# Expert rows gathered in four pieces and turned on VectorE, in a fused attention and mixture-of-experts kernel

## The chip, the cores and the metric

The kernel runs on one core of a Trainium2 chip. The metric is the device time of one execution in microseconds (us). Five engines work beside each other and meet through semaphores: TensorE (PE; its weight loads are listed as PEld), VectorE (DVE), ScalarE (ACT), GpSimd (POOL) and SyncE (SP, which only issues transfers). Each engine runs its own instructions strictly in the order written. Transfers issued by SP, ACT and POOL share 16 DMA engines.

## The reference

```python
# q, k, v, f_logit: (4, 8, 768, 48); w_gate: (384, 8); w1: (8, 384, 1024); w2: (8, 1024, 384)
f = 1 / (1 + exp(-f_logit))
for t in range(S):                     # per batch and head
    state = f[t][:, None] * state + outer(k[t], v[t])
    y[t] = q[t] @ state
x = y.transpose(0, 2, 1, 3).reshape(3072, 384)

logits = x @ w_gate
# all (token, expert) pairs by falling logit: a token goes to the expert if it has
# none yet and the expert has fewer than 384 tokens
for e in range(8):
    out[assigned == e] = relu(x[assigned == e] @ w1[e]) @ w2[e]
```

All inputs and outputs are fp32. Each of the eight experts ends with exactly 384 tokens, that is three tiles of 128 rows.

## The kernel before

**Attention.** 24 chunks of 128 tokens go through a software pipeline whose order is written out by hand (`stages`, `drain`, `finale`). For each chunk the result `x` (128 tokens by 384 features) is written with its eight logits to a table `xd` in DRAM: one row per token, `DX` = 392 columns. POOL copies the logits into the row (`with_logits`, L369), and a store follows (`store`, L374), on SP's queue for 21 chunks and on ACT's for the last three. The steps called through `later(step, ...)` set constants up beside the pipeline.

**The first assignment.** `search` finds, digit by digit, the logit above which each expert takes its first choices. Before it starts, the weights of experts 0 and 1 are asked for (`load_weights`, L576); the small copy before each load ("behind") keeps the load from starting early.

**Lists.** `positions`, `numbers` and `sort` turn the choices into lists of token numbers: a sort is 24 matmuls against one-hot tiles. The list of expert 0's first two tiles is made alone (`tok0`, L895); two indirect DMAs on POOL's queue gather those rows (`fetch`, L769). Then POOL copies `blk` (L900), and VectorE and TensorE make all other lists (`found`, `tok`, L902 to L904). POOL gathers the logits of the tokens left over (`lg`, L914, six transfers) and then the first two tiles of experts 1 to 4 (L920). `idle_turns` are matmuls on constants whose result nobody reads.

**Experts and search, interleaved.** `ffn(e, first_block, n)` gives a list of TensorE pieces: `turn` transposes a row tile by three matmuls into PSUM (L704) and copies it to `xT` (L708, ScalarE except for one tile); `up` makes H = w1 x and its Relu (L716, L720); `down` makes O from `hT` and w2 (L730), copies it (L735) and scatters it to the output with an indirect DMA (L736). At the Relu of `ft` 1 and 6, `up` also asks for the weights of the expert after next. `add` puts the transposes of the next expert among the last down pieces of the one before, `AHEAD_OF` from the end. The pieces stand in a queue `pe_work`. The assignment of the tokens left over (six rounds of `search_rest`, four digits each, with a count on TensorE at L805 and short VectorE operations) is written down beside it: `V` adds a planned duration to VectorE's clock, and `PE` pops pieces until TensorE's planned clock has passed VectorE's, and only then writes the count. So the interleaving is fixed when the program is built, by planned durations. First come two tiles each of experts 0 to 4, under the search; then the third tile of each; then experts 5 to 7 with three tiles each.

Of the kernel before, what the change touches and what calls it, by code (L numbers as in the profile page):

```python
# [25 lines left out]
def kernel(  # L26
# [11 lines left out]
    nc = tc.nc  # L38
# [36 lines left out]
    DX = D + E  # L75
# [292 lines left out]
    def with_logits(G):  # L368
        nc.gpsimd.tensor_copy(out=G["x"][:, D:DX], in_=logits[:, G["b"] * NCH + G["c"]])  # L369

# [85 lines left out]
    later(3, lambda: make_upper_triangular(nc, upper[:], val=1.0, diag=False))  # L456
    later(4, lambda: nc.vector.tensor_copy(out=linef[:], in_=line_i[:]))
# [111 lines left out]
    def load_weights(e, pool, slot, parts=(0, 1), behind=None):  # L569
        for part in parts:  # L570
            shape, src = (([128, DC, F], moe_w1), ([128, FC, D], moe_w2))[part]
            w = pool.tile(shape, FP32, name=f"w{part + 1}", tag=f"w{part + 1}_{slot}", bufs=1)
            if behind is not None:
                (nc.gpsimd.tensor_copy if e < 2 else nc.scalar.copy)(
                    out=w[0:1, 0, 0:1], in_=behind)
            nc.sync.dma_start(out=w[:], in_=src[e].rearrange("(c p) f -> p c f", p=128))  # L576
            slots.setdefault(e, [None, None])[part] = w
# [72 lines left out]
    with tc.manual_schedule(engines=FIXED):  # L650
        for load, n in ((load_f, 0), (load_k, 0), (load_q, 0), (load_f, 1), (load_v, 0), (load_k, 1),
                        (load_q, 1), (load_f, 2), (load_v, 1)):
            load(chunks[n])
        load_gate()
        for z in range(2):
            nc.sync.dma_start(out=mask[HC * z:HC * z + HC, 1], in_=mask[HC - HC * z:C - HC * z, 0])
        attention(-1, ALL)
        for e in range(2):
            load_weights(e, early, e, behind=chunks[-1]["y0"][0:1, 0, 0:1])
        base = search(over0[:], choice0, NT)  # L660
# [4 lines left out]
    def fast():  # L665
# [28 lines left out]
        def ffn(e, first_block, n, ahead=None):  # L694
# [5 lines left out]
            def turn(i):  # L700
                def go():
                    X = bank("Xe", "H")
                    for d in range(DC):
                        nc.tensor.transpose(out=X[:, 128 * d:128 * d + 128],  # L704
                                            in_=rows[e, first_block + i][:, 128 * d:128 * d + 128],
                                            identity=ident[:])
                    copy = nc.vector.tensor_copy if first_block + i == 1 and e == 0 else nc.scalar.copy
                    copy(out=xT[:, :, 128 * i:128 * i + 128],  # L708
                                   in_=X[:, 0:D].rearrange("p (c t) -> p c t", t=128))
                return 0.65, go  # L710

            def up(ft, d):
                def go():
# [5 lines left out]
                    if d == DC - 1:  # L719
                        nc.scalar.activation(out=hT[:, ft, 0:w], in_=L["H"][:, 0:w], func=AF.Relu)  # L720
                        if ahead is not None and ft in (1, 6):
                            load_weights(ahead, pools[ahead], ahead, (ft // 6,),
                                         hT[0:1, ft, 0:1])
# [23 lines left out]
        AHEAD_OF = 3  # L747
# [18 lines left out]

        def fetch(e, i):
            t = work.tile([128, DX], FP32, name="xe", tag="xe", bufs=10)
            nc.gpsimd.indirect_dma_start(  # L769
                out=t[:], out_offset=None, in_=xd[:, :],  # L770
                in_offset=bass.IndirectOffsetOnAxis(ap=token(e, i), axis=0))
            rows[e, i] = t
# [108 lines left out]
        with tc.manual_schedule(engines=engines):  # L881
# [6 lines left out]
            idle_turns(12, "A")  # L888
            p0 = place_of(0, 0)
            r, in_line = sort(line, numbers(blk, value[:], blocks[:, p0:p0 + 2], NT, 2), NT, 2, 4)  # L890
            idle_turns(20, "A")
# [4 lines left out]
            for i in range(2):  # L896
                lists[0, i] = tok0[:, i:i + 1]
                fetch(0, i)
            blk_all = rt([NT], "blk_all", FP16, 1)
            nc.gpsimd.tensor_copy(out=blk_all[:], in_=blk[:])  # L900
            r, _ = sort(line, numbers(blk_all, value[:], blocks[:], NT, NQ), NT, NQ, 12, in_line)
# [5 lines left out]
               float(1024 * (DX // E) + D // E), ALU.add)  # L907
            for e in range(1, NA):
                for i in range(2):
                    p = place_of(e, i)  # L910
                    lists[e, i] = tok[:, p:p + 1]
# [9 lines left out]
            idle_turns(3, "A")  # L921

            clock.update(pe=4.0, dve=0.0)
            for e in range(NA):
                add(ffn(e, 0, 2, e + 2 if e + 2 < NA else None))
                if e == 0:
                    for _ in range(8):
                        piece()

            val_l = rt([NL], "val_l", FP16, 1)  # L930
            nc.vector.tensor_copy(out=val_l[:], in_=found[:, 0:NL])
# [17 lines left out]
            clock["dve"] = 16.8  # L949
# [46 lines left out]
            numb2 = numbers(blk2, val_l[:], blocks[:, NL:NQ, 0:NL], NL, NQ - NL)  # L996
# [5 lines left out]
            ts(tok2[:], sum2[:], 1024.0, ALU.add)  # L1002
            for e in range(E):
                for i in range(2 if e < NA else 0, TE):
                    p = place_of(e, i) - NL
                    lists[e, i] = tok2[:, p:p + 1]
# [30 lines left out]
            for e in range(NA, E):  # L1037
                at = max(0, len(pe_work) - 28)
                pe_work.insert(at, (0.0, lambda e=e: [fetch(e, i) for i in range(TE)]))
# [427 lines left out]
```

## Time and profile before

| What | Value |
|---|---|
| Time, median of 3 runs | 438.8 us (438.66 to 438.98) |
| The profiled execution | 441.33 us, span 439.5 us |
| Mean granted TensorE clock | 0.971 |
| PE busy | 419.9 us, 4576 instructions |
| DVE busy | 184.1 us, 621 instructions |
| POOL busy | 109.7 us, 235 instructions |
| Indirect DMA to gather row tiles (L769) | 24, 966 ns each on POOL |
| Transposes of row tiles on PE (L704) | 72 |
| Attention | to about 139 us |
| First expert matmul (L716) | 164.55 us |

The span runs from the first to the last instruction of the profiled execution. A line in a group names source line, engine, operation, output and input; behind it stand the count, the busy time and the mean duration, and then what the engine waited for before it. The chain of waits is followed back from the last instruction: each step names what released it. The granted clock is the share of full speed that TensorE was given. Busy time on PE is no measure of the work in it, because matmuls overlap: a duration in the chain counts, one in a group is longer.

### The profile page before, as it was taken

What the parts mean: (1) busy time and instruction counts of PE and PEld (TensorE: products, weight loads), DVE (VectorE), ACT (ScalarE), POOL (GpSimd) and SP (SyncE); (2) the same over time, 40 slices, a digit from 0 to 9 for tenths busy, and PEclk for the clock granted to TensorE, in tenths of its full rate; (3) what the DMA queues carried; (4) which work ended last, traced back from release to release, by engine and by line L of the source; (5) the groups of instructions that cost most, each with busy time, mean ns of one, the idle gap of its engine ahead of it and who ended that gap; (6) DMA issues with size and microseconds to landing.
All of it is one profiled execution on the core that took longest, in us unless ns stands there. A gap on an engine that the chain in (4) does not pass through costs nothing.

```text
span 439.5 us, 11007 instructions
## 1 busy us (share of the span) xinstructions
PE 419.9 (96%) x4576; PEld 305.1 (69%) x4576; DVE 184.1 (42%) x621; ACT 157.5 (36%) x370; POOL 109.7 (25%) x235
## 2 busy tenths in 40 slices
PE   7899999999999879999999999999999999999991
PEld 3678888788787558686767777788886556556550
DVE  5598888888898822366666640000000000000000
ACT  3677777677763102121312122232222212203200
POOL 4344444444432037300001032100033014010010
PEclk9999999999999588999999999999999999999997
DMA  9899998798893954845260013079932102000010
GB/s 156 141 175 178 187 190 181 167 185 182 175 195 104 398 206 146 307 148 171 91 221 36 1 42 89 36 244 294 318 104 67 38 18 70 22 18 36 1 37 22
DMA packets 119147, 59.31 MB, mean 135 GB/s; under 512 B 102320, under 2 KB 113712, under 8 KB 119088
## 3 DMA queue, kind: packets, MB, share of 16 engines
q1 hardware_dynamic: 115392, 48.35, 44.0%
q0 software_dynamic: 3264, 9.56, 6.8%
q8 instruction: 38, 0.62, 0.6%
q10 hardware_dynamic: 432, 0.60, 0.4%
q14 instruction: 21, 0.17, 0.2%
HBM read 48.91 MB, written 9.54 MB: 133 GB/s over the span
## 4 chain that ended last, share of the span: by engine, by line
PE 69%; issue 15%; DMA 6%; DVE 3%; POOL 3%; ACT 2%; SPq 0%; POOLq 0%; DVEq 0%
PE H L716 23%; PE O L730 21%; PE T L234 4%; DMA w<-in_moe_w_dram 4%; PE A L276 3%; PE L L171 3%; PE Y L306 3%; PE L L361 2%; PE T L344 2%; PE small L255 2%; PE Xe L704 2%; PE Y L317 1%; POOL out_dram L736 1%; DMA q<-in_q_dram 1%; PE small L199 1%
## 5 line engine op out<-in xcount | busy, mean ns | idle before, releaser
L716 PE MATMUL H<-xeT,w 128*128 128x256 f32 (+2 forms) x624 | 132.7, 370 | 0.8 <-issue 0.8
L730 PE MATMUL O<-w,hT 128*128 128x384 f32 x384 | 132.6, 490 | 0.0
L716 PEld LDWEIGHTS H<-xeT,w 128*128 128x128 f32 x624 | 100.4, 193 | 27.7 <-ACT xeT L708 1.1
L730 PEld LDWEIGHTS O<-w,hT 128*128 128x128 f32 x384 | 69.7, 190 | 39.2 <-issue 0.2
L736 POOL DMA_INDIRECT out_dram<-o,tok x24 | 23.3, 970 | 211.5 <-ACT o L735 206.1
L720 ACT ACTIVATE hT<-H 128x256 f32<-128x256 f32 (+2 forms) x104 | 38.2, 367 | 91.3 <-PE H L716 87.9
L735 ACT COPY o<-O 128x384 f32<-128x384 f32 x24 | 11.5, 478 | 74.5 <-PE O L730 73.0
L284 DVE COPY_PREDICATED am<-mask,A 128x512 f32<-128x512 int32 x48 | 34.6, 724 | 0.2 <-PE A L276 0.2
L708 ACT COPY xeT<-Xe 128x384 f32<-128x384 f32 x23 | 11.0, 478 | 55.5 <-PE Xe L704 55.5
L769 POOL DMA_INDIRECT xe<-xd,tok x24 | 23.2, 966 | 19.7 <-DMA w<-in_moe_w_dram 12.7
L276 PE MATMUL A<-qT,kT 48*64 48x128 f32 (+1 forms) x768 | 22.3, 251 | 0.4 <-ACT kT L242 0.3
L171 PE MATMUL L<-g,wcum 128*128 128x384 f32 x48 | 19.7, 491 | 1.0 <-ACT g L167 1.0
L306 PE MATMUL Y<-am,v 64*64 64x64 f32 (+1 forms) x368 | 19.8, 243 | 0.0
L276 PEld LDWEIGHTS A<-qT,kT 48*64 48x64 f32 x768 | 18.7, 133 | 1.4 <-ACT kT L242 0.5
L157 POOL COPY w<-v 64x256 f32<-64x256 f32 x48 | 18.9, 394 | 2.5
L306 PE MATMUL Y<-am,w 64*64 64x128 f32 (+1 forms) x368 | 19.2, 243 | 0.0
L306 PEld LDWEIGHTS Y<-am,v 64*64 64x64 f32 x368 | 17.9, 134 | 0.0
L234 PE MATMUL T<-ident,qg 128*128 128x128 f32 x96 | 15.8, 285 | 2.2 <-DVE qg L187 2.0
L344 PEld LDWEIGHTS T<-ident,yT 128*128 128x128 f32 x92 | 11.6, 150 | 8.8 <-ACT qT L242 5.6
L209 POOL TENSOR_TENSOR gl<-span,spans 128x4 f32<-128x4 f32 x20 | 3.9, 196 | 54.2 <-DVE span L206 33.2
L306 PEld LDWEIGHTS Y<-am,w 64*64 64x64 f32 x368 | 17.3, 134 | 0.0
L176 DVE TENSOR_SCALAR dl<-L 128x384 f32<-128x384 f32 x24 | 13.3, 554 | 8.8 <-PE L L171 8.4
(238 smaller groups left out, 543.4 us busy)
## 6 DMA issues: line engine op xcount, KB each, us to landing
w<-in_moe_w_dram SPq DMA_DIRECT2D x16, 1536.0 KB, 7.8
f<-in_f_logit_dram SPq DMA_DIRECT2D x24, 192.0 KB, 4.2
k<-in_k_dram SPq DMA_DIRECT2D x24, 192.0 KB, 5.1
q<-in_q_dram SPq DMA_DIRECT2D x24, 192.0 KB, 4.9
v<-in_v_dram SPq DMA_DIRECT2D x24, 192.0 KB, 4.8
xd<-x SPq DMA_DIRECT2D x21, 196.0 KB, 4.5
xd<-x ACTq DMA_DIRECT2D x3, 196.0 KB, 6.4
xe<-xd,tok POOLq DMA_INDIRECT x24, 3.5
```

What stands on the lines that cost most here:

```text
L157: nc.gpsimd.tensor_copy(out=w[HC * z:HC * z + HC], in_=G["v"][HC - HC * z:C - HC * z, H // 2:H])
L171: nc.tensor.matmul(out=G["Lv"], lhsT=wcum[:], rhs=g_bufs[G["i"] % NB][:, :, 0:DH], start=True, stop=True)
L234: nc.tensor.transpose(out=t[:, 128 * hp:128 * hp + 128], in_=G[src][:, 2 * hp:2 * hp + 2, :].rearrange("t h d -> t (h d)"), identity=ident[:])
L276: nc.tensor.matmul(out=A[par][to, 128 * hp + first * j:128 * hp + 128], lhsT=G["kT"][rows, hp, HC * j:HC * j + HC], rhs=G["qT"][rows, hp, ...
L284: nc.vector.copy_predicated(am[:, par].rearrange("s (a b) t -> s a b t", b=2), mask[:].unsqueeze(2).to_broadcast((128, 2, 2, 128)), A[par] ...
L306: nc.tensor.matmul(out=G["Y"][r0][DP * r:DP * r + DP, 128 * blk + first:128 * blk + 128], lhsT=v, rhs=G["am"][rows, h % 2, h // 2, first:128],
L344: nc.tensor.transpose(out=X[:, 128 * hp:128 * hp + 128], in_=G["yT"][:, hp, :], identity=ident[:])
L716: nc.tensor.matmul(out=L["H"][:, 0:w], lhsT=slots[e][0][:, d, 128 * ft:128 * ft + 128], rhs=xT[:, d, 0:w], start=(d == 0), stop=(d == DC - 1))
L720: nc.scalar.activation(out=hT[:, ft, 0:w], in_=L["H"][:, 0:w], func=AF.Relu)
L730: nc.tensor.matmul(out=L["O"][:, 0:D], lhsT=hT[:, ft, 128 * i:128 * i + 128], rhs=slots[e][1][:, ft, :], start=(ft == 0), stop=(ft == FC - 1))
L736: nc.gpsimd.indirect_dma_start(out=outs[next(tiles)][:, :], out_offset=bass.IndirectOffsetOnAxis(ap=token(e, first_block + i), axis=0), in ...
L769: nc.gpsimd.indirect_dma_start(out=t[:], out_offset=None, in_=xd[:, :], in_offset=bass.IndirectOffsetOnAxis(ap=token(e, i), axis=0))
```

## The change

A row tile is no longer gathered as 128 whole rows. The table's rows become 480 columns wide, five pieces of 96: four pieces of features and one of logits, the eight logits repeated twelve times, so that a row can be addressed in pieces. For a tile, four indirect DMAs fetch 128 pieces each. A new list (`quadrants`: four short matmuls with `perm` and one VectorE operation) names for each partition the token and the piece: in gather g, partition 32a + r gets piece a of token 32g + r. Then VectorE's transpose, which works within blocks of 32 by 32, gives the full transpose of the tile in four instructions (`by_blocks`). The features land in the order 3p + d, so the first weights are loaded with three neighbouring rows on a partition ("(p c) f"). Expert 0's first two tiles are still gathered whole and transposed by matmul (`by_matmul`), in the same order of features, and are worked on one after the other instead of together. The lists of all others are made from `blk` directly, without POOL's copy, before expert 0's transposes. The numbers of idle turns, `AHEAD_OF`, the planned start of the search (16.8 to 14.0) and the places of the later fetches change with it, and the copies before weight loads touch all 128 partitions.

```diff
-    DX = D + E
+    PW = D // 4
+    DX = 5 * PW
...
-        nc.gpsimd.tensor_copy(out=G["x"][:, D:DX], in_=logits[:, G["b"] * NCH + G["c"]])
+        nc.gpsimd.tensor_copy(
+            out=G["x"][:, D:DX].rearrange("t (n e) -> t n e", e=E),
+            in_=logits[:, G["b"] * NCH + G["c"]].unsqueeze(1).to_broadcast((128, PW // E, E)))
...
+    perm = const([128, 4, 128], FP16, "perm")
+    first_piece = const([128, 1], FP32, "first_piece")
+    for a in range(4):
+        later(8 + a, lambda a=a: nc.gpsimd.memset(first_piece[32 * a:32 * a + 32], 5120.0 + a))
+        later(9 + a, lambda a=a: nc.gpsimd.tensor_copy(
+            out=perm[:, a].rearrange("p (b r) -> p b r", r=32),
+            in_=ident[:, 32 * a:32 * a + 32].unsqueeze(1).to_broadcast((128, 4, 32))))
...
-                    out=w[0:1, 0, 0:1], in_=behind)
-            nc.sync.dma_start(out=w[:], in_=src[e].rearrange("(c p) f -> p c f", p=128))
+                    out=w[:, 0, 0:1], in_=behind)
+            nc.sync.dma_start(out=w[:], in_=src[e].rearrange(
+                "(p c) f -> p c f" if part == 0 else "(c p) f -> p c f", p=128))
...
             def turn(i):
-                def go():
-                    X = bank("Xe", "H")
+                def by_matmul():
+                    X = [bank("Xe", "H"), bank("Xe2", "O")]
+                    x = rows[e, first_block + i][:, 0:D].rearrange("t (p d) -> t d p", d=DC)
                     for d in range(DC):
-                        nc.tensor.transpose(out=X[:, 128 * d:128 * d + 128],
-                                            in_=rows[e, first_block + i][:, 128 * d:128 * d + 128],
-                                            identity=ident[:])
-                    copy = nc.vector.tensor_copy if first_block + i == 1 and e == 0 else nc.scalar.copy
-                    copy(out=xT[:, :, 128 * i:128 * i + 128],
-                                   in_=X[:, 0:D].rearrange("p (c t) -> p c t", t=128))
-                return 0.65, go
+                        nc.tensor.transpose(
+                            out=X[d > 0][:, 128 * d:128 * d + 128], in_=x[:, d],
+                            identity=ident[:])
+                    nc.vector.tensor_copy(out=xT[:, 0, 0:128], in_=X[0][:, 0:128])
+                    nc.scalar.copy(out=xT[:, 1:DC, 0:128],
+                                   in_=X[1][:, 128:D].rearrange("p (c t) -> p c t", t=128))
+
+                def by_blocks():
+                    x = rows[e, first_block + i][:, 0:D].rearrange(
+                        "t (g c d) -> t g d c", g=4, d=DC)
+                    for g in range(4):
+                        nc.vector.transpose(
+                            out=xT[:, :, 128 * i + 32 * g:128 * i + 32 * g + 32], in_=x[:, g])
+                    V(4, 0.25)
+
+                return (0.65, by_matmul) if e == 0 and first_block < 2 else (0.0, by_blocks)
...
-        AHEAD_OF = 3
+        AHEAD_OF = 8
...
         def fetch(e, i):
-            t = work.tile([128, DX], FP32, name="xe", tag="xe", bufs=10)
-            nc.gpsimd.indirect_dma_start(
-                out=t[:], out_offset=None, in_=xd[:, :],
-                in_offset=bass.IndirectOffsetOnAxis(ap=token(e, i), axis=0))
-            rows[e, i] = t
+            if e == 0 and i < 2:
+                t = rows[e, i] = work.tile([128, DX], FP32, name="x0", tag="x0", bufs=2)
+                nc.gpsimd.indirect_dma_start(
+                    out=t[:], out_offset=None, in_=xd[:, :],
+                    in_offset=bass.IndirectOffsetOnAxis(ap=token(e, i), axis=0))
+                return
+            t = rows[e, i] = work.tile([128, D], FP32, name="xe", tag="xe", bufs=7)
+            for g in range(4):
+                nc.gpsimd.indirect_dma_start(
+                    out=t[:, PW * g:PW * g + PW], out_offset=None,
+                    in_=xd[:, :].rearrange("n (a x) -> (n a) x", x=PW),
+                    in_offset=bass.IndirectOffsetOnAxis(ap=quads[e, i][g], axis=0))
+
+        def quadrants(found16, n, name):
+            PE(0.1)
+            r = bank("quad", "r")
+            for g in range(4):
+                nc.tensor.matmul(out=r[:, g * n:g * n + n], lhsT=perm[:, g], rhs=found16,
+                                 start=True, stop=True)
+            q = rt([4, n], name, I32, 1)
+            ts(q[:].rearrange("p g n -> p (g n)"), r[:, 0:4 * n], 5.0, ALU.mult,
+               first_piece[:, 0:1], ALU.add)
+            return q
...
-            idle_turns(12, "A")
+            idle_turns(11, "A")
...
-            idle_turns(20, "A")
+            idle_turns(6, "A")
...
-            blk_all = rt([NT], "blk_all", FP16, 1)
-            nc.gpsimd.tensor_copy(out=blk_all[:], in_=blk[:])
-            r, _ = sort(line, numbers(blk_all, value[:], blocks[:], NT, NQ), NT, NQ, 12, in_line)
+            r, _ = sort(line, numbers(blk, value[:], blocks[:], NT, NQ), NT, NQ, 12, in_line)
...
+            found16 = rt([NQ], "found16", FP16, 1)
+            nc.vector.tensor_copy(out=found16[:], in_=found[:])
+            idle_turns(6, "A")
+            quad = quadrants(found16[:], NQ, "quad")
+            idle_turns(6, "A")
...
-            idle_turns(3, "A")
-
             clock.update(pe=4.0, dve=0.0)
             for e in range(NA):
-                add(ffn(e, 0, 2, e + 2 if e + 2 < NA else None))
-                if e == 0:
-                    for _ in range(8):
+                ahead = e + 2 if e + 2 < NA else None
+                if e:
+                    add(ffn(e, 0, 2, ahead))
+                else:
+                    add(ffn(e, 0, 1, ahead))
+                    add(ffn(e, 1, 1))
+                    for _ in range(16):
                         piece()
...
-            clock["dve"] = 16.8
+            clock["dve"] = 14.0
...
+            sum16 = rt([NQ - NL], "sum16", FP16, 1)
+            nc.vector.tensor_copy(out=sum16[:], in_=sum2[:])
+            V(4)
+            quad2 = quadrants(sum16[:], NQ - NL, "quad2")
...
             for e in range(NA, E):
-                at = max(0, len(pe_work) - 28)
-                pe_work.insert(at, (0.0, lambda e=e: [fetch(e, i) for i in range(TE)]))
+                for i in range(TE):
+                    at = max(0, len(pe_work) - 64 + 12 * i)
+                    pe_work.insert(at, (0.0, lambda e=e, i=i: fetch(e, i)))
                 add(ffn(e, 0, TE))
```

## The prediction

> **What bounds the kernel now.** I read the page's busy times first, then the chain of work that ended last, then the granted clock microsecond by microsecond where the chain leaves TensorE, then VectorE's groups.
>
> The busy times of the span of 439.5 us:
>
> ```profile
> PE 419.9 (96%) x4576; PEld 305.1 (69%) x4576; DVE 184.1 (42%) x621; ACT 157.5 (36%) x370; POOL 109.7 (25%) x235
> ```
>
> The chain, in order of time (start, length, what):
>
> ```profile
> 140.23 15.94 DMA w<-in_moe_w_dram
> 156.32 1.18 POOL xe L769
> 157.81 0.95 POOL xe L769
> ...
> 160.16 1.51 PE tokens L874 x24
> 161.68 0.84 PE nothing L106 x3
> 162.52 1.28 PE Xe L704 x6
> 163.80 0.75 issue
> 164.55 4.78 PE H L716 x12
> ...
> 291.78 5.36 PE H L716 x48
> 297.13 3.87 PE O L730 x12
> 301.33 1.29 PE O L730 x4
> 302.63 5.36 PE H L716 x48
> ```
>
> From 164.55 us on, the chain is TensorE alone: every TensorE piece taken out shortens the kernel by its length, if nothing else becomes late. Between 140 and 164.55 us it is a hand-over: weight loads and the last stores of rows, the first gather, the sort that gives all other lists, then the six transposes. An fp32 matmul stands as two records, a transpose as one. The expert from 291.78 to 302.63 takes 10.85 us: 5.35 us for 24 up matmuls (223 ns each), 16 down records at 3.87/12 = 0.3225 us, that is 5.16 us, and a rest of 0.33 us: the three transposes of the next tile, put among the down matmuls.
>
> TensorE by microsecond (busy and count, granted clock, DMA share, GB/s):
>
> ```profile
> 158.00:159.00 1.00, 0.20 (x2) 1.00 1.09 356
> ...
> 161.00:162.00 1.00, 1.00 (x16) 0.83 0.01 3
> ...
> 168.00:169.00 1.00, 1.00 (x5) 0.75 0.07 2
> ```
>
> TensorE has nothing from 158.2 to 160.16; the clock falls to half in 161 and is full again only in 168. The first 12 up records therefore take 398 ns each, later ones of this width 227 (8 in 1.82 us): 2.05 us lost.
>
> VectorE's groups by form (count | busy, mean ns | idle before):
>
> ```profile
> L206 DVE STREAM_TRANSPOSE span<-small 128x128 f32<-128x128 f32 x24 | 7.4, 308 | 0.0
> L426 DVE TENSOR_SCALAR full_r<-cnt,there 128x32 f32<-128x32 f32 x24 | 6.0, 251 | 23.8 <-PE cnt L805 23.8
> ...
> L816 DVE STREAM_TRANSPOSE turned<-most_r 128x32 f32<-128x32 f32 x24 | 5.1, 211 | 0.8
> ```
>
> In the search (180 to 258 us) VectorE waits for TensorE, 23.8 us over 24 digits, mostly 0.43 us each: that is the room for more VectorE work.
>
> **The change part by part.** The sum is made against the span of 439.5 us; the profiled execution itself took 441.33 us, the median of the runs shown is 438.8, so I take the difference from 438.8.
>
> *Transposes off TensorE.* Of 24 row tiles, two (expert 0's first two) are still transposed by matmul. 22 x 0.33 us = 7.3 us leave the chain: eight tiles of experts 1 to 4, five third tiles, nine of experts 5 to 7. Their ScalarE copies go too (478 ns each, off the chain). **-7.3.**
>
> *VectorE's side.* Four transposes of 128x96 a tile. Between the two rows (211 ns for 32 columns, 308 for 128) one is about 275 ns; independent instructions start closer than their length (0.12 us apart at 200.10 and 200.22, of 0.21 us), so a tile takes 0.85 to 1.1 us; the planner counts 1.0. Eight tiles fall into the search, in four pairs, and the planner puts more TensorE pieces before each next count. Cost 0; without that room the bound is 8 x 0.1 = 0.8, and if the reads with a step of three elements cost double, 32 x 0.25 = 8 less 4 x 4 x 0.43 = 7 of room around the pairs, so about 1. After 260 us VectorE is idle.
>
> *Four gathers a tile.* An indirect DMA holds POOL 0.95 us, the next starts 0.3 later, whatever the row size: 1.25 us. Rows are gathered by POOL in the order lg, experts 1 to 4, and only then the scatters. With lg from about 159.4 us (below), six lg end at 166.9, eight pieces for expert 1 start until 175.6, and land 2.6 later in quiet (lg: 2.2 to 3.3), 7.3 at most beside a weight load (the slowest xe): 178 to 183. Who waits: VectorE's transposes of expert 1 stand behind round 1's sums, and behind them stand the next round's operations, its count on TensorE, and expert 1's matmuls. By TensorE's order the round's fourth count comes at 179.5 us (162.5, 24 ups 5.36, transposes 0.33, 8 downs 5.16, 2 + 21 ups 5.1, four counts 0.6, the rest waits), the sums 2.5 later at 182, expert 1's first matmul at 185. So the gathers are there or about 1 late, with 1 us of room: I take +0.3, between 0 and +1.5. Experts 2, 3, 4 have their pieces by 189, 199, 209 us and start at about 208, 230, 252. The scatters of expert 0 wait until POOL is through, 207 us: then three o buffers are held, and the fourth ScalarE copy (208 us) waits some 1.5 us, behind it the Relu of expert 2; three banks of H cover 2 us: 0. Of the later lists, expert 0's third tile is nearest: from the second quadrant product 0.5 us to the list, 3.75 to the fourth issue, 2.9 to land and turn, 7.5 in all, against 16 downs = 10.3 us: 0, with 3 us left.
>
> [...] The row first: lg's 32-byte rows land in 2.2 to 3.3 us, xe's 1568-byte rows in 3.0 at best, so small pieces are not slower here. [...] I take 0.
>
> *A full list beside the first gathers.* Before, the all-lists product waits for POOL's small copy behind both gathers (158.76), and expert 0's transposes stand behind it on TensorE. After, VectorE forms it from 155.33 to 156.5, the sort is through at 158.0, the lists at 158.9, the quadrant product, and TensorE is free at about 160.5 after 12 idle turns. The end is then the first gather: it lands 4.9 us after its issue at 156.32. That issue waited for the last row store (token list ready at 155.3, so 0.7 us is the store's); a store is 480 columns instead of 392, 22% more: its 6.6 us to landing grow by 0 to 1.45, I take 0.4, since the weights queued with it set most. Landing 161.6; one transpose, the small VectorE copy (about 0.3) and hand-overs make the first up matmul 162.5 instead of 164.55: 2.05 us, less 0.33 for the second tile's transposes now inside. **-1.7** (0 to -3).
>
> *The clock.* By the rows above, 2 us without a matmul and then 1.5 us of narrow ones sufficed for half clock. After, the longest hole is about 1.2 us, with twelve idle turns at 158 to 160.5. [...] by the strict row it drops again and, starting earlier, stays down up to 6 us: 0 to +1. [...] **-2.05.**
>
> *Small terms.* Expert 0 one tile at a time: 48 ups of 223 ns against 24 of 454, **-0.2**; a quadrant product of four short matmuls in the stream, like a count of six (0.15), **+0.1**. The second tile's VectorE copy now stands behind lg's work: the last lg starts at 165.7, expert 2's weights are now asked for at 164.5 (the Relu that triggers them is early), so landing is 168 to 172.3, the chain behind it 2.0 us (172.15 to 174.17) and the copy 0.3, against a need at 173.4: 0 to 1.2, **+0.3**. Attention: 24 stores of 44 KB more, at 390 GB/s 2.7 us of DMA time beside a DMA share of 0.91; the loads run steps ahead and the waits for them sum to 5 us, so 0 to +2.7, **+0.5**. The wider copy on POOL (205 to about 300 ns), the setup of perm, the copies of 128 partitions and the first weights' other layout lie on idle engines or behind prefetch: 0.
>
> Sum, with the 0.3 for expert 1's gathers: -7.3 - 1.7 - 2.05 - 0.2 + 0.1 + 0.3 + 0.5 + 0.3 = -10.05: **428.8 us** (429.5 us of span).
>
> **Rivals.**
> 1. *The start gains little* (clock falls again, or the first gather lands with the old transposes): +2.05 to +3 on the sum, **431.5 us**. For it: half clock held from 141 to 154 through much short work. Against it: the idle turns.
> 2. *VectorE or the attention stage pays*: transposes with stepped reads at double cost, or stores that DMA cannot hide, +2.7 to +5, **433 us**. Against it: VectorE's 0.43 us per digit.
> 3. *Slower: late pieces stall VectorE in order*, with the search and TensorE behind. Place: expert 1's transposes. It takes away the gain from the point where its last piece lands 11 us after 183, which needs an issue interval of about 2.7 us instead of 1.25; at 3 us the last start is 188, landing 193 to 195, and with expert 2's pieces 24 us later than planned it would be about **443 us**. For it: 32 gathers in a row on one queue[...]. Against it: all 30 gathers seen took 0.94 to 1.18 us[...].
> 4. *The work only moves* (TensorE idle where transposes were, as the next matmul waits for VectorE): the 7.3 us stay, **436 us**. Against: tiles are turned eight pieces (4 us) ahead.
>
> **How the numbers follow.** Forecast 0.52, rival 1 0.25, rival 2 0.13, rival 4 0.04, rival 3 0.06. The forecast's own range is 427 to 430.5. The range for 8 in 10 takes in rivals 1 and 2 as far as 434, and downwards a start 2 us better than taken. A measurement of this kernel tells about 0.2% from no change (438.66 to 438.98 seen). Faster 0.92, same 0.02, slower 0.06.
>
> **What would show it.** Right: no TensorE transposes after 175 us, an expert of one tile in 10.5 us, first up matmul near 162.5 us at clock 1.00, VectorE transposes of about 275 ns or less, search end with TensorE unbroken. Wrong: VectorE idle on a DMA between 180 and 260 us, TensorE waiting for xeT from VectorE, half clock after 162 us, an attention stage that ends after 139 us.

## The result, and the profile after

The changed kernel takes 433.1 us (431.0 to 433.88, 4 runs) against 438.73 us before (438.17 to 438.98): ratio 0.986, 95% interval 0.983 to 0.989. The prediction said 428.8 us. Faster was right, and the time lies in the range for 8 in 10, which went up to 434, but above the forecast's own 427 to 430.5. That it fell in the wider range is luck: the part above 430.5 was there for rivals 1 and 2, and what happened is neither. The profiled execution took 431.0 us, the fastest of the four, with a span of 429.2 us.

The busy times of the changed kernel:

```profile
PE 410.2 (96%) x4560; PEld 299.7 (70%) x4560; DVE 207.2 (48%) x713; ACT 149.5 (35%) x357; POOL 175.1 (41%) x308
```

TensorE lost 9.7 us of busy time; VectorE gained 23 us and GpSimd 65 us, and both are still busy for less than half of the span.

The chain of waits of the changed kernel (start, length, what):

```profile
155.68 3.78 DMA x<-xd,tok
159.69 0.95 POOL lg L962
160.94 0.94 POOL lg L962
...
164.68 7.49 DMA lg<-xd,at_l
174.56 0.76 PE H L737 x4
175.49 3.16 PE H L737 x14
178.78 1.66 PE H L737 x14
...
277.26 5.36 PE H L737 x48
282.62 5.16 PE O L751 x16
287.78 5.36 PE H L737 x48
```

Two things are to be seen. From 277 us on, an expert of one tile takes 287.78 - 277.26 = 10.52 us instead of 10.85: the transposes are gone from the chain. But the chain leaves TensorE a second time: at 164.68 us the last of the six gathers of `lg` takes 7.49 us to land, where the kernel before had TensorE unbroken from its first up matmul on. Then 14 up records take 3.16 us, and the next 14 take 1.66.

TensorE by microsecond (busy and count for PE, PEld, DVE, ACT and POOL, then granted clock, DMA share, GB/s):

```profile
161.00:162.00 1.00, 1.00 (x11) 1.00 (x11) 0.00 (x0) 0.28 (x1) 0.88 (x1) 1.00 0.10 4
...
169.00:170.00 1.00, 1.00 (x5) 0.60 (x4) 0.00 (x0) 0.00 (x0) 0.70 (x2) 1.00 0.77 7
...
172.00:173.00 1.00, 0.00 (x0) 0.00 (x0) 0.64 (x3) 0.15 (x1) 0.84 (x1) 1.00 1.06 393
...
176.00:177.00 1.00, 1.00 (x7) 1.00 (x7) 0.90 (x4) 0.28 (x1) 0.92 (x1) 0.50 0.59 193
```

The clock stays at 1.00 through the first up matmuls, as forecast, and falls to half only at 175.1 us, after the hole that ends at 174.56 us.

VectorE and TensorE in order of time around the hole (start, length, engine, line, operation, what it waited for):

```profile
166.31 5.33 PE L751 MATMUL O<-w,hT 128*128 128x384 f32 x16
174.56 0.76 PE L737 MATMUL H<-xeT,w 128*128 128x128 f32 x4 [2.93 <-DVE xeT L719]
```

```profile
172.29 0.31 DVE L429 TENSOR_SCALAR lg<-lg,low_scale 128x48 f32<-128x48 f32 x1 [7.29 <-DMA lg<-xd,at_l]
...
174.22 0.28 DVE L719 COPY xeT<-Xe 128x128 f32<-128x128 f32 x1
```

TensorE waits 2.93 us for the copy of expert 0's second tile (L719). That copy is short and its input is ready at about 166.5 us; it stands on VectorE behind the work on `lg`, and that work waits for the gather.

VectorE's groups by form (count | busy, mean ns | idle before):

```profile
L727 DVE STREAM_TRANSPOSE xeT<-xe 128x96 f32<-128x96 f32 x88 | 22.4, 288 | 85.0 <-DMA xe<-xd,quad 59.6 <-PE H L737 23.0 <-PE O L751 2.4
...
L429 DVE TENSOR_SCALAR full_r<-cnt,there 128x32 f32<-128x32 f32 x24 | 6.0, 251 | 20.7 <-PE cnt L850 20.7
```

A transpose of 128x96 takes 288 ns on average, and in the order of time eight in a row (two tiles) take 1.63 us, 0.2 us each. VectorE still waits 20.7 us for the counts (23.8 before). Between 175 and 262 us it waits for no piece; its waits for pieces (59.6 us) come after that and cost nothing: but for 0.2 us at the very first, TensorE waits for `xeT` only in the hole.

The gathers (count, median us from issue to landing):

```profile
xe<-xd,quad POOLq DMA_INDIRECT x88, 2.5
```

Whole rows of 1568 bytes took 3.5 us before. Pieces of 384 bytes, at 2.5 us, are no slower to land.

### The profile page after: what moved, and what is told of

It reads as the page before. It is cut to its first block, busy times and chain, and to the rows that moved or that the text cites. A ratio compares the mean times of both kernels' runs of the same rounds, so it can differ in the third digit from the quotient of the medians.

```text
span 429.2 us, 11122 instructions
## 1 busy us (share of the span) xinstructions
PE 410.2 (96%) x4560; PEld 299.7 (70%) x4560; DVE 207.2 (48%) x713; ACT 149.5 (35%) x357; POOL 175.1 (41%) x308
## 4 chain that ended last, share of the span: by engine, by line
PE 61%; issue 19%; POOL 10%; DVE 5%; DMA 3%; ACT 1%; POOLq 0%; DVEq 0%
PE H L737 16%; PE O L751 15%; POOL xe L799 6%; PE T L235 5%; PE A L277 4%; PE L L172 4%; PE Y L307 3%; POOL out_dram L757 3%; PE L L362 2%; PE T L345 2%; PE small L256 2%; PE Y L318 2%; DMA lg<-xd,at_l 2%; PE small L200 2%; PE T L107 1%
## 5 line engine op out<-in xcount | busy, mean ns | idle before, releaser
L737 PE MATMUL H<-xeT,w 128*128 128x128 f32 (+2 forms) x672 | 134.1, 356 | 3.1 <-DVE xeT L719 3.1
L751 PE MATMUL O<-w,hT 128*128 128x384 f32 x384 | 128.9, 489 | 0.0
L737 PEld LDWEIGHTS H<-xeT,w 128*128 128x128 f32 x672 | 102.7, 194 | 29.1 <-DVE xeT L719 3.9
L751 PEld LDWEIGHTS O<-w,hT 128*128 128x128 f32 x384 | 71.3, 190 | 44.7
L799 POOL DMA_INDIRECT xe<-xd,quad x88 | 83.4, 948 | 36.2 <-issue 25.9
L741 ACT ACTIVATE hT<-H 128x128 f32<-128x128 f32 (+2 forms) x112 | 39.6, 354 | 92.4 <-PE H L737 91.1
L727 DVE STREAM_TRANSPOSE xeT<-xe 128x96 f32<-128x96 f32 x88 | 22.4, 288 | 85.0 <-DMA xe<-xd,quad 59.6
```

The costliest lines, as they stand in the source:

```text
L727: nc.vector.transpose(out=xT[:, :, 128 * i + 32 * g:128 * i + 32 * g + 32], in_=x[:, g])
L737: nc.tensor.matmul(out=L["H"][:, 0:w], lhsT=slots[e][0][:, d, 128 * ft:128 * ft + 128], rhs=xT[:, d, 0:w], start=(d == 0), stop=(d == DC - 1))
L751: nc.tensor.matmul(out=L["O"][:, 0:D], lhsT=hT[:, ft, 128 * i:128 * i + 128], rhs=slots[e][1][:, ft, :], start=(ft == 0), stop=(ft == FC - 1))
L799: nc.gpsimd.indirect_dma_start(out=t[:, PW * g:PW * g + PW], out_offset=None, in_=xd[:, :].rearrange("n (a x) -> (n a) x", x=PW), in_offse ...
```

## The experiments

The experiments are named by the first letters of their labels (e1 to e8; a b marks a second run). Their ratios are to the kernel before, run beside them.

**The changed kernel again, and the suspected cause taken away.** The suspicion: expert 2's weights are asked for by the Relu of `ft` 1 and 6. Since expert 0's tiles are worked on one by one, these come at 162.6 and 166.0 us, while the last three `lg` gathers (issued at 162.2, 163.4 and 164.7 us) are under way. The two issues stand in one merged line of the changed kernel:

```profile
162.59 3.82 SPq L586 DMA_DIRECT2D w<-in_moe_w_dram  x2
```

First the same kernel again, then one edit (e2): the second tile asks instead of the first.

```diff
-                    add(ffn(e, 0, 1, ahead))
-                    add(ffn(e, 1, 1))
+                    add(ffn(e, 0, 1))
+                    add(ffn(e, 1, 1, ahead))
```

> The changed kernel as it is, for a second profile beside the first. In the first, TensorE stood still from 171.6 to 174.56 us, because the second tile's VectorE copy stands behind the work on the left-over logits, which landed at 172.2, and then ran at half clock until 178.7. Theory A (expert 2's first weights, now asked for at about 162 us, hold the last logit gathers up): the hole is there again, 2 to 5 us, with half clock behind it, and the time is 431 to 434. Rival B (the hole was that execution's accident, and something else makes the median 2 us slower than the first profile): no hole of over 1 us, time the same.

> Only the place where expert 2's weights are asked for is moved, from the Relus of expert 0's first tile to those of its second, some 10 us later. Theory A: the logit gathers land about 2.5 us after their issue, by 168 us, the hole of 3 us and the half clock behind it (1.5 us more) go, 428 to 429.5 us; the weights then run beside expert 1's pieces, which may cost 0 to 1 us at expert 1's transposes. Rival B (the gathers are slow among themselves, 38 of them in a row on one queue): the hole stays, 433.

The kernel again: 432.29 us against 439.29 before in the same set, ratio 0.984 (0.979 to 0.990), with the hole again:

```profile
175.92 1.22 PE L737 MATMUL H<-xeT,w 128*128 128x128 f32 x4 [3.85 <-DVE xeT L719]
...
177.14 2.85 PE L737 MATMUL H<-xeT,w 128*128 128x128 f32 x14
```

With the weights one tile later: 426.85 us, ratio 0.973 (0.968 to 0.978). Run once more on another chip, beside e7b below:

> The kernel with the weights asked for one tile later, again, beside the one without turns on the same chip: ratio to before 0.968 to 0.978, no hole before the second tile, first up matmul at 160 to 162 us at full clock. If the gain of 5.4 us over the changed kernel came from the chip of that run, it is 0.98 or more.

426.43 us against 439.28, ratio 0.971 (0.967 to 0.975). In its order of time on TensorE and VectorE:

```profile
166.37 5.33 PE L751 MATMUL O<-w,hT 128*128 128x384 f32 x16
171.53 0.61 PE L737 MATMUL H<-xeT,w 128*128 128x128 f32 x4
...
172.13 1.81 PE L737 MATMUL H<-xeT,w 128*128 128x128 f32 x14
```

```profile
168.35 0.31 DVE L429 TENSOR_SCALAR lg<-lg,low_scale 128x48 f32<-128x48 f32 x1 [3.31 <-DMA lg<-xd,at_l]
...
170.28 0.28 DVE L719 COPY xeT<-Xe 128x128 f32<-128x128 f32 x1
```

VectorE waits 3.31 us for `lg` instead of 7.29 to 8.12, the copy is done 0.97 us before TensorE starts on it, and the hole is gone. The edit moves only weight loads, and it is worth 432.29 - 426.85 = 5.4 us. The trace accounts for it: 3.85 us of hole, and 1.65 us more for the next 18 up records at half clock (1.22 + 2.85 us against 0.61 + 1.81). The weights' collision with `lg` is shown to be the cause; how a load delays a gather inside the DMA engines is not. This is also the fastest version of the study. Whether it would do as well to take the copy off VectorE's queue was not run.

**Which of the two loads.** The first weights still in the first tile, the second in the second tile:

```diff
...
-                    add(ffn(e, 0, 1, ahead))
-                    add(ffn(e, 1, 1))
+                    add(ffn(e, 0, 1, ahead, (1,)))
+                    add(ffn(e, 1, 1, ahead, (6,)))
```

The new argument lists the values of `ft` whose Relu asks. It ran twice; the first set is told below.

> The changed kernel with the two weights of expert 2 parted: the first one still asked for in the first tile (at 162.4 us), the second only in the second tile. Theory A1, the first one alone is in the way of the last gathers of lg (it is asked for before they start): the hole before the second tile stays at 2 us or more, time 430.5 to 432.5. Theory A2, the second one (asked for at 165.9, as the last gather starts) is what delays them: no hole, 426.9 within 1 us. Between: both share it.

> The same kernel as e8 (expert 2's first weights asked for in the first tile, its second weights in the second), run again, since in e8 all engines but GpSimd stood still for tens of microseconds while GpSimd issued its gathers, and two thirds of the landing records of its queues were missing. If that came from the chip of that run: about 427 to 432, with no such standstill, and then the question of e8 is answered: a hole of 2 us or more before the second tile and 430.5 to 432.5 if the first weights alone are in the way of lg; no hole and 426.9 within 1 us if it is the second. If it came from the edit: 498 again.

429.31 us, ratio 0.975 (0.970 to 0.981), halfway between e1 and e2, and a hole of 1.6 us:

```profile
174.81 0.71 PE L737 MATMUL H<-xeT,w 128*128 128x128 f32 x4 [1.60 <-DVE xeT L719]
175.36 0.30 PE L850 MATMUL cnt<-above_r,in_line 128*128 128x32 f16 x6
175.51 1.81 PE L737 MATMUL H<-xeT,w 128*128 128x128 f32 x14
```

Neither theory has it alone. By the trace, the six `lg` gathers land after 2.5, 2.2, 2.4, 6.8, 7.9 and 7.5 us in the changed kernel, after 2.8, 2.3, 2.4, 6.7, 6.8 and 6.1 us with the first weights alone, and after 2.6, 2.3, 2.4, 2.8, 3.2 and 3.4 us in e2b, where both come later. So the first load, asked for 0.3 to 0.4 us behind the issue of the fourth gather, makes most of the delay of these landings, and the second adds 0.1 to 1.4 us. In e3 below, where one load falls among the gathers, the last two land after 6.3 and 6.7 us. The price is shared out otherwise: the last microsecond of delay lengthens the hole from 1.6 to 2.93 us (3.85 in e1), and only behind the longer hole does the clock fall; here 14 records take 1.81 us. Of the 2.9 us that e8b takes more than e2b, the hole is 1.6. In its profiled execution the start was 1.5 us later too (first up matmul at 161.92 us); that lies ahead of the edit's place, and what makes up the rest in the median is open.

**The wider rows alone.** The kernel before with `DX` = 480 and the repeated logits, and nothing else but one gather buffer less (9 instead of 10).

```diff
-    DX = D + E
+    PW = D // 4
+    DX = 5 * PW
...
```

> The kernel before with rows of 480 columns alone (the logits repeated twelve times, nine instead of ten buffers for gathered tiles); gathers, lists and transposes as before. The forecast's term: stores 22% larger cost 0 to 2.7 us in the attention stage, taken as 0.5, so 439.3. Rival: rows of 1920 bytes[...] land sooner than rows of 1568 (in the two profiles a store on SP's queue took 3.2 us to landing instead of 4.5), the attention stage waits less for its loads, 437.3 to 438.3.

439.54 us, ratio 1.000 (0.998 to 1.003): 22% more to store in the attention stage cost nothing that can be measured, and the rival's gain of 1 to 2 us is not there either: a store on SP's queue takes 4.6 us to landing there, against 4.5 before.

**The tiles turned on TensorE again.** The changed kernel, with all tiles gathered whole and transposed by matmul, with ScalarE's copy.

```diff
-                return (0.65, by_matmul) if e == 0 and first_block < 2 else (0.0, by_blocks)
+                def by_rows():
+                    X = bank("Xe", "H")
+                    x = rows[e, first_block + i][:, 0:D].rearrange("t (p d) -> t d p", d=DC)
+                    for d in range(DC):
+                        nc.tensor.transpose(out=X[:, 128 * d:128 * d + 128], in_=x[:, d],
+                                            identity=ident[:])
+                    nc.scalar.copy(out=xT[:, :, 128 * i:128 * i + 128],
+                                   in_=X[:, 0:D].rearrange("p (c t) -> p c t", t=128))
+
+                return (0.65, by_matmul if e == 0 and first_block < 2 else by_rows)
...
```

> The changed kernel with the tiles of experts 1 to 7 and all third tiles gathered as whole rows by one transfer again and transposed by matmul, in the same order of features, each three transposes and one ScalarE copy; lists, expert 0, weights and the rest as changed. The forecast's term: 22 tiles x 0.33 us = 7.3 slower than the changed kernel, 440.3. Rival (part of the gain is given back in the search by VectorE's transposes and by late pieces): only 3 to 5 slower, 436 to 438. The quadrant products stay in it and cost 0.1.

443.25 us, ratio 1.009 (1.005 to 1.012), 11 us above e1 instead of 7.3. Its chain:

```profile
282.05 5.36 PE H L746 x48
287.40 0.65 PE O L760 x2
288.05 0.34 PE Xe L735 x3
288.39 4.52 PE O L760 x14
292.91 5.36 PE H L746 x48
```

A tile's transposes cost 0.34 us there, 22 x 0.34 = 7.5 us, as in the prediction's first term. The rest of the span's 10.8 us is not in the matmuls: the first up matmul comes 0.9 us later (161.72 against 160.78; the idle turns ran at half clock), and 2.5 us lie behind the last scatter. That second part was new, and the next experiment follows it.

**The end of the kernel.** From the start of the last scatter to the end of the span, nothing is left but its landing and GpSimd's closing. In before, e3 and e4 this took 8.0, 7.9 and 7.9 us, in the changed kernel and e2 5.6 us. The first three start 54 indirect DMAs, the others 120. The experiment adds 55 small gathers, whose result nobody reads, to the kernel before: seven behind each one-tile expert, ten behind experts 5 and 6.

```diff
...
+            def more(n):
+                def one(i):
+                    extra = work.tile([128, E], FP32, name="extra", tag="extra", bufs=8)
+                    nc.gpsimd.indirect_dma_start(
+                        out=extra[:], out_offset=None,
+                        in_=xd[:, :].rearrange("n (a e) -> (n a) e", e=E),
+                        in_offset=bass.IndirectOffsetOnAxis(ap=at_l[:, i:i + 1], axis=0))
+                pe_work.extend([(0.0, lambda i=i: one(i % NL)) for i in range(n)])
...
```

> The kernel before with 55 extra gathers of 128 rows of 32 bytes into a tile that nobody reads, put into GpSimd's order in the last 170 us (seven behind each of the five one-tile experts, ten behind experts 5 and 6), so that it starts 109 indirect DMAs instead of 54. From the start of the last scatter to the end of the span lie 8.0, 7.9 and 7.9 us in the three kernels with 54 indirect DMAs (before, the wide rows alone, turned by matmul) and 5.6, 5.4 and 5.6 us in those with 120 (the changed kernel twice, weights later). Theory D, the number of indirect DMAs decides how long GpSimd takes to close: the end is 5.5 us and the time is 2.4 us shorter than before (0.9945), although work was added. Rival E, something else in the pieces decides it: the end stays 7.9 us, the time is the same within 0.5 us.

The expectation of theory D failed in its sign. The last scatter in e5's order of time on GpSimd:

```profile
457.48 0.96 POOL L736 DMA_INDIRECT out_dram<-o,tok  x1 [4.18 <-ACT o L735]
```

The span ends at 470.1 us, 12.6 us after that start and not 5.5. In the trace's records GpSimd's closing drain instruction has one length for each of the three numbers of indirect DMAs, the same in all runs of the table:

| Indirect DMAs | Kernels | Drain | Last scatter to end |
|---|---|---|---|
| 54 | before, e3, e4, e6b | 4.489 us | 7.9 to 8.1 us |
| 109 | e5 | 8.981 us | 12.6 us |
| 120 | the changed kernel, e1, e2, e2b, e7b, e8b | 1.222 us | 5.4 to 5.8 us |

From 54 to 109 that is (8.981 - 4.489) / 55 = 0.082 us for each DMA. At 120 it is what 14 would cost at that price; why is open. So the end does not follow "more is shorter", and the changed kernel gained 2.4 us there. The 109 come from the set at the end of this section, but in that set e6, e7 and e8 show the drains of their numbers, 4.489, 1.222 and 1.222 us. Only three numbers were run, and the kernels with 120 differ from e5 in more than the number, so that the number alone makes their drain short is not shown. (The time of e5, 463.08 us against 443.27, isn't used, and it was not run again.)

**The lists beside the first gathers, alone.** The kernel before with this part of the change only:

```diff
-            blk_all = rt([NT], "blk_all", FP16, 1)
-            nc.gpsimd.tensor_copy(out=blk_all[:], in_=blk[:])
-            r, _ = sort(line, numbers(blk_all, value[:], blocks[:], NT, NQ), NT, NQ, 12, in_line)
+            r, _ = sort(line, numbers(blk, value[:], blocks[:], NT, NQ), NT, NQ, 12, in_line)
```

The idle turns are 11, 6 and 12 instead of 12, 20 and 3.

> The kernel before with one part of the change alone: the product for all lists is formed from VectorE's own tile beside the first gathers, the small copy on GpSimd is gone, and the idle turns are placed as in the changed kernel (11, 6 and 12 instead of 12, 20 and 3). Prediction: first up matmul 1.7 to 2 us earlier than 164.55 (162.5 to 162.8), and at full clock another 2 us where the kernel before had half: ratio 0.991 to 0.996. Rival, the first gather's landing sets the first matmul either way: 0.5 us at most, ratio 0.999 to 1.

> The same kernel as e6 (the kernel before with the lists' product beside the first gathers alone), run again for the same reason: e6's first up matmul came 2.6 us earlier than before's, but ScalarE then waited 5.6 and 6.6 us for TensorE, which stood still. If that came from the chip: ratio 0.991 to 0.997 by the prediction's 1.7 to 2 us (and up to 2 more where the clock holds), 0.999 to 1 by the rival that the first gather sets the start either way. If it belongs to the edit: 1.01 again.

438.22 us against 439.49, ratio 0.997 (0.995 to 0.999), by the ratio 1.45 us less. The first up matmul comes at 162.38 us, 12.76 us after the first idle turns of that stage (149.62) instead of 164.55 - 150.19 = 14.36. The prediction's mechanism for the start holds. The clock still falls: the first 12 up records take 4.51 us, against 4.78 before and 2.83 at full clock in e3.

```profile
162.38 4.51 PE L716 MATMUL H<-xeT,w 128*128 128x256 f32 x12 [0.85 <-ACT xeT L708]
```

**Without the idle turns.** The kernel e2 without the two times six idle turns around the quadrant product.

```diff
-            idle_turns(6, "A")
             quad = quadrants(found16[:], NQ, "quad")
-            idle_turns(6, "A")
```

> The kernel with the weights asked for one tile later (426.85 us), without the twelve idle turns around the quadrant product. If the turns hold the clock, as the prediction had it, the first up matmuls run at half clock: 12 of them in 4.8 us instead of 2.7, and the time is 1.5 to 2.5 us longer (428.4 to 429.4). If they don't: 426.9 within 0.6, and the first up matmul is no earlier, since the first gather sets it.

> The same kernel as e7 (weights one tile later, without the twelve idle turns around the quadrant product), run again beside the kernel with the turns, since e7's standstill was not seen again in e8's kernel on another chip. If the turns hold the clock, as the prediction had it: first 12 up records in 4.5 to 4.8 us instead of 2.7 or less, and 1.5 to 2.5 us more than the kernel with the turns. If they don't matter: the same within 0.6 us, the first up matmul not earlier, since the first gather sets it.

429.73 us, ratio 0.978 (0.974 to 0.983), 3.3 us more than e2b in the same set and more than the 1.5 to 2.5 expected. In order of time on TensorE, and two microseconds of its clock:

```profile
159.95 0.88 PE L716 MATMUL Xe<-ident,x 128*128 128x128 f32 x3 [2.18 <-DMA x<-xd,tok]
160.84 5.84 PE L737 MATMUL H<-xeT,w 128*128 128x128 f32 x30
```

```profile
159.00:160.00 1.00, 0.05 (x1) 0.08 (x1) 0.00 (x0) 0.00 (x0) 0.95 (x1) 0.50 0.67 169
...
164.00:165.00 1.00, 1.00 (x7) 1.00 (x6) 0.00 (x0) 0.11 (x1) 0.94 (x1) 0.50 0.12 4
```

And the same place in e2b:

```profile
159.61 0.58 PE L716 MATMUL Xe<-ident,x 128*128 128x128 f32 x3 [0.98 <-issue]
160.40 3.64 PE L737 MATMUL H<-xeT,w 128*128 128x128 f32 x30 [0.21 <-DVE xeT L719]
```

The clock falls to half inside the gap of 2.18 us, at 158.7 us, for some 7 us, and the same 30 records take 5.84 instead of 3.64 us. With the turns the gap is 0.98 us, and the clock stays. In this pair the turns do hold it: the mean granted clock is 0.976 to 0.978 in the four runs without them and 0.983 to 0.984 in the four with them.

**A set that isn't used.** e5, e6, e7 and e8 first ran together on one chip: 463.08, 447.96, 498.46 and 498.0 us, against 443.27 before there. In these traces all engines but GpSimd stand still for long stretches while GpSimd issues its gathers (in e8 TensorE waits 11.66 us in one place), and 38 to 68% of the landing records of GpSimd's queues are missing. The kernels of e6, e7 and e8, run again on other chips, show none of it and take 438.22, 429.73 and 429.31 us. So it doesn't belong to their edits. Whether it is the chip or the taking of the records, no run here shows.

## Why the prediction was right or wrong

| Step | Taken | Measured | From |
|---|---|---|---|
| Transposes off TensorE | -7.3 | -7.5 | e4: 22 x 0.34 |
| VectorE's transposes | 0 | 0 | TensorE never waits for them; 0.2 us each |
| Pieces for expert 1 | +0.3 | 0 | no wait of TensorE for `xeT` after 175 us |
| Lists beside the first gathers, and one tile first | -1.7 | -1.45 and -0.7 | e6b; and below |
| Clock at the first up matmuls | -2.05 | at most about -1.4 | the runs of before, below |
| Attention's stores | +0.5 | 0 (-1.1 to +1.1) | e3 |
| Second tile's copy behind `lg` | +0.3 | +5.4 | e1 against e2 |
| GpSimd's closing | not in the sum | -2.4 | the table above |

The measured terms make -8.1 us; the first pair gave -6.1 (-7.3 to -4.8), and e1 against before -7.0 (-9.4 to -4.6). Without the collision they make -13.5, and e2 and e2b measured -12.4 and -12.85. So the terms are 0.6 to 2 us too large together. They come from different kernels and can overlap; which one is too large is open.

**Where it failed.** The step was "the second tile's VectorE copy now stands behind lg's work", costed at +0.3 from a range of 0 to 1.2. Its mechanism is what the trace shows: an early Relu asks for the weights, the last `lg` gather lands late, and the copy is queued behind. Its term was mis-sized in three places. The last gather landed at 164.68 + 7.49 = 172.17 us: at the upper end of the 168 to 172.3 that the prediction had itself written down, where it took a value near the lower end. TensorE needed the copy at 171.6 us and not at 173.4, because the first up matmul came at 160.35 instead of the 162.5 from which 173.4 was reckoned (162.5 + 5.36 + 0.33 + 5.16); the `lg` gathers began only 1 us earlier than reckoned (158.44 instead of 159.4). And the price of a gap was its length alone; after 2.93 us the clock halved, which added another 1.65 us. The trace before had warned of it: the clock was at half behind its gap of 2 us. Two of the prediction's own signs of being wrong are there: TensorE waits for `xeT` from VectorE, and the clock is at half after 162 us. The same kernel with the loads moved is 426.4 to 426.9 us.

**The start.** Besides the lists, one tile at a time helps: from the first transpose to the first up matmul it is 1.85 us in e6b (six transposes, then a ScalarE copy of 384 columns) and 0.80 in the changed kernel, 1.05 us less; the second tile's 0.34 us of transposes come later, which leaves -0.7. In the profiled pair the start gained 4.2 us, but 1.3 of these were the attention stage ending earlier in that execution. One reading of the prediction was wrong here. It put 0.7 us ahead of the first gather (156.32 us) down to the last row store; but in the trace before, that store had landed by 154.62 us, ahead of the token list (155.3). GpSimd then needs 0.9 us from the end of its last wait to the gather's start, and so it does in the changed kernel (154.78 to 155.68 us), where the list is early (153.98) and the store, landed at 154.58 us, does come last.

**The clock.** The prediction read 2.05 us off the one profiled execution and subtracted it from the median. The 51 runs of the kernel before that went with e1, e8b and e7b fall into three groups by mean granted clock: 0.983 to 0.984 with about 438 us (16 runs), 0.979 to 0.980 with 439.3 (19), and 0.971 to 0.976 with 441.2 (16). The profiled execution had 0.971, so it was one of those that lose most, and the median run loses only some 1.4 us: there was no more to gain. Profile against profile shows -10.3 us and the medians -5.6, since the profiled execution of before lies 2.6 us above its median and that of the changed kernel 2.1 us below its own. The direction was right, and e7b shows that without the idle turns the clock is lost.

That the clock would stay up at a longest hole of about 1.2 us, with twelve idle turns, was an estimate of the author's. At the start of the changed kernel it held: the longest gap there was 0.94 us, and the first up matmuls ran at 1.00. Against that, the clock fell with gaps of 2.18 (e7b) and 2.93 us (the changed kernel). What the prediction read in the trace before, half clock after 2 us without a matmul and 1.5 us of narrow ones, is nearer, but no limit either. In e8b the clock fell at 157.3 us, where the longest gap of TensorE had been 0.46 us and 24 narrow matmuls of a sort ran (busy and count of PE, PEld, DVE, ACT and POOL, granted clock, DMA share, GB/s); in e4 it was the same at 157.1 us.

```profile
157.00:158.00 1.00, 1.00 (x18) 0.85 (x15) 0.06 (x1) 0.00 (x0) 0.65 (x1) 0.67 1.06 399
158.00:159.00 1.00, 1.00 (x5) 0.46 (x4) 0.51 (x4) 0.00 (x0) 0.70 (x2) 0.50 0.46 167
```

In e3, on the other hand, the clock stayed up through a gap of 2.00 us, where the kernel before lost it with one of 1.97 us (PE alone, granted clock, DMA share, GB/s):

```profile
158.00:159.00 1.00, 0.00 (x0) 1.00 0.85 219
...
162.00:163.00 1.00, 0.44 (x2) 1.00 0.00 0
```

So the length of a gap does not decide alone. The stretches at half clock between 138 us and the last matmuls last 13.7 and 6.8 us in the kernel before, 10.2 and 3.4 us in the changed one, and the one from 158.7 us in e7b lasts 6.8 us. By an estimate from these lengths, 3.4 or 6.8 us at half clock take 1.7 or 3.4 us of TensorE's time, near the 1.3 and 3.2 us by which the second and third group of the kernel before lie above the first. What sets the lengths, why a gap of 2 us costs nothing in one execution and a stretch at half clock in another, and how much work keeps the clock up, no run here shows.

**The rivals.** Rival 2 named 433 us, which is nearly the time, but for VectorE's transposes or the attention stage, and both cost nothing. Rival 1, a start that gains little, is ruled out by 160.35 us at full clock. Rival 3 needed gathers 2.7 us apart; they came 1.25 us apart, from 165.93 to 204.73 us, and the scatters began at 205.97 us, against 207 in the prediction. Rival 4 would have left a one-tile expert at 10.85 us. None of them contained the case that came true; one of the forecast's own small terms did.

## What to carry to other kernels

When a change moves the start of a stage, cost its waits at the early end of that start too, with every deadline and every trigger moved along: here a Relu that came early pulled 3 MB of weights beside the last three of six small gathers, and that took back 5.4 us of about 12.5. Don't put a short copy that TensorE needs behind work that waits for a transfer on the same engine, and when it has to stand there, take the upper end of the landing and add the clock that a gap costs (1.65 us in e1, behind 3.85 us). And read what a profiled execution lost to the clock against the spread of the runs, before it is counted as a gain.

## What the runs showed of the hardware

- Small gathers (128 rows of 32 bytes) land in 2.2 to 3.4 us (before, e2b), in 6.1 to 6.8 us beside one weight load of 1.5 MB (e8b, e3) and in 6.8 to 8.4 us beside two (the changed kernel, e1). In that time the DMA engines were busy to 0.77 while moving only 7 GB/s (169 to 170 us of the changed kernel).
- The clock fell to half with gaps on TensorE of 2.0 (before), 2.2 (e7b) and 2.9 us (the changed kernel), but also with none over 0.46 us among narrow matmuls (e4, e8b), and stayed up through one of 2.0 us in e3. It came back after 3.4 and 10.2 us in the changed kernel, after 6.8 and 13.7 us in the kernel before and after 6.8 us in e7b.
- GpSimd's closing drain took 4.49 us after 54 indirect DMAs, 8.98 us after 109 (0.082 us for each one more), and only 1.22 us after 120.
- VectorE's block transposes of 128x96 fp32, with reads that step by three elements, take 288 ns on average and start 0.2 us apart in a row.
